# Two-bank projections, key feature sums on TensorE and table loads set by the order, in a gated mix of an S4 convolution and linear attention

## The chip, the cores and the metric

One core of a Trainium2 chip runs the whole program. The metric is the device time of one execution in microseconds (us), of which three runs of the kernel before are given. Engines are named as in the profile: PE (TensorE), DVE (VectorE), ACT (ScalarE), POOL (GpSimd), and SP, whose queue issues nearly all DMAs.

## The reference

Two operators read the same input `x = A_u` (1 x 2048 x 512, bf16) and a gate mixes them. Cut to what is computed:

```python
# A: S4 convolution, per channel d with 128 complex states n
logdA = dt * (A_re + 1j*A_im);  dB = dt * (B_re + 1j*B_im);  Cc = C_re + 1j*C_im
K = einsum("dn,dnl,dn->dl", Cc, exp(logdA[:, :, None] * l), dB).real      # kernel of length 2048
a = irfft(rfft(pad(x)) * rfft(pad(K)))[:2048] + x * Dskip

# B: linear attention, 32 heads of 16 features, "hedgehog" feature map
q, k, v = split(x @ wqkv);  pq = q @ w_phi;  pk = k @ w_phi               # per head
phi = concat([softmax(p), softmax(-p)])                                   # 32 features
num = phi_q @ (phi_k^T v);  den = phi_q . sum_s(phi_k) + 1e-6
b = (num / den) @ wo

g = sigmoid((x * gate_w).sum(-1));   out = g * a + (1 - g) * b
```

## The kernel before, in words

Everything is one program in which each piece of work is a node of a plan (`Plan.add`): an engine, a name, a function that emits its instructions, the nodes that it depends on, and the buffer rings that it takes and drops. `Plan.run` (L153) emits the nodes in a written order. `ORDER` is a string of two-character node numbers, `SIDES` says for each node with a choice whether ACT or DVE does it (evictions of PSUM mostly), and `RINGS` which of two PSUM rings it takes. Each engine executes its instructions in the emitted order; semaphores between engines follow from the tiles.

The work has these stages, which the order interleaves.

1. Tables (`prepare`). Parameters and `x` are loaded on the SP queue; sines and cosines for the Fourier stages (`tgs`, `sine`), transposed `x` (`xps`, `xT`), key and query weights folded with `w_phi` (`wtp`, `wps`, `fold`), and the convolution's tables C, D and G: exponentials `p_d`, `p_ce`, `p_g`, then four rounds of sines (`trig4`: `p_fc` or `p_fd`, `p_ab`, two `p_sn`), joined on DVE (`p_pr`, `p_px`, `p_dd`, `p_de`).
2. Spectrum of `x` (`keys_and_spectrum`): copies `udc`, first stage `psAu` with evictions `XAu`, second stage `psBu` with evictions `XU`, written to DRAM (`xuw`).
3. Keys (`attention_keys`), eight steps `s2` of two token tiles `u`. For each tile `pk` projects the keys into one PSUM bank (128 x 512), two exponentials `ek` (plus and minus) write `Ek`; the sums over the 16 features of each head come either by PE and a DVE reduction or by a DVE reduction alone (`zp`, `zk`, the string `ZPS` chooses; four steps each); `rz` takes the reciprocal as exp(-ln); `vp` projects the values, `vb` evicts them, `vr` multiplies by the reciprocal, and `kn` adds key times value into `kvp`. `kvbd` (L785 to L795) then writes the block-diagonal `KVbd`.
4. Queries (`block`), four blocks of 512 tokens: projection `pq`, exponentials `eq`, sums `zs`, a chain `z1` to `z5`, the weights to DRAM and back, spread over partitions (`aw`, `ar`), multiplication `em` on DVE (L913), `ops` with `KVbd`, eviction `oT`. Blocks 0 to 2 use one-bank tiles of the ring `bk`; block 3 (`late`) runs two banks at a time.
5. Convolution (`plan_conv`), 16 units of 32 channels. Sines `cs` (from `argC`) come in phases of four units with a load of the sine set before and of the exponential set after. Per unit: exponential `E` and its copy `El`, tables A (`A1`, `A2`, and an addition `A3` at L1110 unless `FOURS` has a 1 for the unit, in which case PE adds four terms instead of two), `Rh` and `Rl`, kernel matmuls `kps`, eviction `KD`, Fourier stages `psA`, `psB` with evictions `XA`, `XK`, product `t` (L1231) with the spectrum of `x`, inverse stage `psz`, eviction `Zr`, a turn through DRAM (`zw`, `zr`), last stage `psy`, gating `ou`, and the stores `out`.

[...] The ring `ps` has two tiles of two banks throughout. The other four banks hold `p0` (two wide tiles) in the table stage; then, from the node `x_psum`, the pool `psA` with three one-bank tiles `bk` and one bank `acc`; then, from the node `x_q` (after the last early query block), two wide tiles `pf`. [...]

```python
LN_EXP = "natural_log_exp_and_others"
TRIG = "trig_and_small"
def begin(self, name):                                   # L64
    return self.nc.scalar.preload_act_table_set(name)
```

Loads of a set are nodes of their own here (`tabT`, `tabL`), with dependencies that keep every sine between them.

Of the kernel before, what the change touches and what calls it, by code (L numbers as in the profile page):

```python
# [43 lines left out]
def build_index_cols(nc, pool):  # L44
    idx_i = pool.tile([128, 1], I32, name="idx_i")
    nc.gpsimd.iota(idx_i[:], pattern=[[0, 1]], base=0, channel_multiplier=1)
    want = (("p", 0, 127), ("p31", 0, 31), ("p63", 0, 63), ("h16", 4, 7), ("h2", 4, 1), ("s5", 5, 3), ("b5", 5, 1), ("b6", 6, 1))
# [23 lines left out]
class Plan:  # L71

    DIGITS = "0123456789abcdefghijklmnopqrstuvwxyzABCDEFGHIJKLMNOPQRSTUVWXYZ-_"
    ORDER = ("040B0H0K0d0y0C0D0L0s0I070J0M0P0g000S110j0N08010z0T0m0Q0e2R0a0p0q0r0_0W2T100U0O0V14120Y2U2x0A2S050k130Z2y2V2X2Z0R190v0t0u"
             "0b0c0w2_0l0E0X2W1516172L1a061b2Y022-30311y33340n030f0-"
             "0h1e1f0i1w2J18321c0F0o2B2K2M1n1z1H1g1A1o2D2C1d1p1I091x1E1J351Q1R2F1B0x1C2E0G2H1q36372G2I2P382N2Q391F3b2O3c4C1S3a4J4L4K4M"
             "3d3e4Q4R3f4U1Y3g4N1r4O1h4V3h1L4Y4-"
             "4P3i4Z4_3j4W4S53542z57504T3k4X1Z515b5d58521s1D593l5c3n5i5e55565j3m5a1G3o5q5f5g5s5r5t3p3r3q1T5m5n5u3s5v5h5o5k5w5x5B1P4D4E"
             "3w2v5l5p4F5y5F5C3y1U5H3x5G5I5J5z5A1V5D5E3t3z5U3D5K5V5M5N3A3R3E2w3F5W5L1O5_3G5O5Q5X5Y5Z3B3C1W605R5S1N3K3M1K3S1M5-"
             "5P3L634G642A615T653N673T6869626a666m6n6o3U6p3V3W3X3Y6b6c6q6d6r6s1t3Z3H3-1X3_3O1i1j41401_4221431-"  # L80
             "1k1l204445466e272923222b282d4748243P491m2a4a2c2e4b4g2f4c2g4d252h2o4e4h4i4n1u4j3u3v2j4p2i2l2k2m2q2p6i262s4q4o1v4k2n4u2r2t"
             "6f4v4w6j4r3I2u4x4y4z6g4l8l3J4A8p8m6t6u6k6v8q3Q4f4s6x6h8k8o6l8n8r8s6y6z6w6A6C4m4t4B8C6G8t6I6K8w8x8y8u6B6H6J4H8D8v6L6M6N7d"
             "8z8A8E4I8B7e7f8I7g8F6F9e8Q8G8H9b6O6P8R7h7j7i6Q6R8J9f7M7N8S6S6T6U6Vaeaf7O8W8X8K7k9g8L8T8U8Z8-"
             "938M8N7l6D8_7m8V7n6W6X6Y8O8P8Y7P94an7o7pao7q6_70717r90917Qa47S9295ag7R6Z7s6-"
             "72aha8a9966Ea7akaca5ai73aa75979998ajap7677a69aalatamab74ad7TaBaC7t797u7v7U78au7y7z7V7w7x9caq9naras7AavaH7W9d9h9o9paw7X9v"
             "aY9waK7Y7ZaDaL9q9raZ7a9x9y9zaIc57B7-aM9kc69D9EaQaEbX9L7Cb_aF7D9M7_9Ac07EaRaG9iaxaz80ay9B818285bYaA7Ga-"
             "7IaJ86879j9Fc19s7Jb-"
             "9l9m9Na_7bc7aNaOaPc3cbb2b37HbZc283aS9C7FaT849G9H9I9t89aUaWaV8baX7cccc8c99O9u9P9Q9R888cb87Kb9b0c4caceb19J8abacfcgbg8dck9K"
             "8ecl8f8gbbbh8hbcbibob4cP9Sbpbqcd9T8ichci7L8jcBcCcjcsdYcYctcucycDczdZd-cQcR9Ucmd_cHcvcw9W9Xcnbj9VbwbkblbxcocIbre0eLcp9Ze1"
             "e2b5b6eMbse3eUeVcxb7bye4cqbtbu9Ybdbe9-"  # L90
             "9_cAcrcSbme5cZdOdScEbfcFcGcTcUe6a0a1bve7dTdRdWeNa2e8cJcKe9bzbAedeecLeRcNcOa3eSeaebeOcMc_ePbBd0ecd1d7cVd8d9cWeCdfcXeWdPdU"
             "d2daefege-e_eQd3dbdQdgeTdVd4dndodXdhdcg1g2dieDeEdjeXbKfAbCbnbDbEbFeYfBeZf0f1bGc-dpbLddg7dqbHd5f2drbMf3f4f5bNfGbIbJbOezdk"
             "eAfDdsfEeBeIf6f7feffdldtbPdebQdBfCfHehdueifFejdmf8fgeJd6ekdvfIfJdyf9fafhfbg4fifKg5g6dwfjdzfkfcdxdCdEfLdAdFfMg3g8dGg9dHfN"
             "fleFelfdfmfpdDdLgagbgcgddIeGemeKfqeHfOfPfQfRgeenepfneofreqeresgfggghgifSfTfUfofsbRgjbSgkdJftetglfVfYfZgmgngobUbVgqfufWdM"
             "dNbWgpf-fvfxfygreufwevewexbTeydKfzfXf_g0gvgwgsgtgugx")
    SIDES = ("011111010010101011001110110010011001010100001011100000000000011000011001111101000100000100000000000000000000000010000000"
             "00100001000000000000000101010000000000000100001101001")
    RINGS = ("001010111111010010100000000000000000000000100000000000000000001101100000000101101011100100100001101010111100111001010100"
             "01111")
    WARM = ("000000000000000000000000000000000000000000000000000000000000000000000000000000000000000000000000000000000000000000000000"  # L100
            "000000000000000000000")
    FOURS = ("0111100101011000")
    ZPS = ("01000111")

    HOT = ("pk", "vp", "pq", "zp", "ops", "bps4", "psA", "psBu", "psB128", "psB64", "psB32", "psz", "pszn", "psyn32", "psy128", "psy64", "psy32", "kps")
# [5 lines left out]
    def add(self, eng, name, fn, deps=(), take=(), drop=(), rw=("", ""), tab=None, sets=None, opens=None, cost=0.0):  # L111
        n = Bag()
        n.eng, n.name, n.fn, n.take, n.drop, n.cost = eng, name, fn, list(take), list(drop), cost
        n.tab, n.sets, n.opens, n.ring = tab, sets, opens, None
# [38 lines left out]
    def run(self):  # L153
        code = {d: i for i, d in enumerate(self.DIGITS)}
        order = [64 * code[a] + code[b] for a, b in zip(self.ORDER[0::2], self.ORDER[1::2])] or list(range(len(self.nodes)))
        assert sorted(order) == list(range(len(self.nodes)))
        sides, rings, warm = iter(self.SIDES), iter(self.RINGS), iter(self.WARM)
        for n in self.nodes:
            n.at = n.eng if isinstance(n.eng, str) else n.eng[int(next(sides, 0))]
            for r in n.take:  # L160
                if not isinstance(r, str):
                    n.ring = r[int(next(rings, 0))]
                elif r in self.psums:
                    n.ring = r
            n.warm = int(next(warm, 0)) if n.name in self.HOT and n.ring in ("ps", "bk", "pf") else 0
        done = set()
# [32 lines left out]
def prepare(P, nc, g, evict, psum):  # L199

    fc, act, persist, at = g.fc, g.act, g.persist, g.at
    F = Bag()
# [8 lines left out]
    def S(name, fn, r="", w="", deps=()):  # L211
        return P.add("ACT", name, fn, deps, rw=(r, w))

    t1 = P.add("ACT", "tabT", lambda: act.begin(TRIG), rw=("", "act"), sets="T")
# [57 lines left out]
    def sine(out, v, kv, w, turn=False):  # L272
        S("tgs", lambda: act(out=out(), in_=(low(v()) if not turn else low(v()).rearrange("p (h t) -> p t h", h=2)), func=ACT.Sin, scale=TURN), r="act " + kv, w=w)
# [11 lines left out]
    for hf in range(2):  # L285
# [5 lines left out]
        S("tgs", lambda hf=hf, i=i: act(out=tb(1, hf), in_=F.v[i][:].bitcast(F32), func=ACT.Sin, scale=-1.0, bias=HALF_PI), r=f"act v{i}", w=f"TB1{hf}")  # L291
# [34 lines left out]
    P.add("ACT", "tabL", lambda: act.begin(LN_EXP), [n for n in P.nodes if n.name == "tgs"], rw=("", "act"), sets="L")  # L326
# [4 lines left out]
    S("dtc", dtc, r="act ldc", w="dtc")  # L331
# [49 lines left out]
    S("p_e", lambda: act(out=Tt(4)[:], in_=g.ld_b[:], func=ACT.Exp), r="act ldb tmp", w="t4")  # L381
# [16 lines left out]
    for b in range(8):  # L398
        S("p_d", lambda b=b: act(out=g.D[:, 0, b, :], in_=are(), func=ACT.Exp, scale=64.0 * (b - 3.5)), r="act t2", w=f"D{b}")
    S("p_g", lambda: act(out=g.G[:], in_=are().unsqueeze(2).to_broadcast([128, 512, 2]), func=ACT.Exp, scale=-32.0), r="act t2", w="G")  # L400
    for a in range(4):
        S("p_ce", lambda a=a: act(out=mag()[:, a, :], in_=are(), func=ACT.Exp, scale=512.0 * a + 255.5), r="act t2", w="t7 t8")
    trg = P.add("ACT", "tabT", lambda: act.begin(TRIG), rw=("", "act"), sets="T")
    def trig4(name, fill, r):
# [3 lines left out]
        S("p_sn", lambda: act(out=F.sc[:, 0], in_=X(), func=ACT.Sin, scale=TURN), r="act B0", w="s0")  # L408
        S("p_sn", lambda: act(out=F.sc[:, 1], in_=N(), func=ACT.Sin, scale=-1.0, bias=HALF_PI), r="act B1", w="s1")
# [53 lines left out]
    def at0(e):  # L463
# [4 lines left out]
        e.tensor_scalar(out=at.mask2[:], in0=c8[:, 0:2], scalar1=icol["h2"], scalar2=None, op0=ALU.is_equal)  # L468
# [15 lines left out]
    def at3(e):  # L484
# [8 lines left out]
        e.tensor_copy(out=SZ[:].rearrange("p (m c) -> p m c", m=4)[:, :, 0:32:4], in_=at.mask8[:].unsqueeze(1).to_broadcast([128, 4, 8]))  # L493
# [66 lines left out]
def keys_and_spectrum(P, nc, g, psum):  # L560
# [3 lines left out]
    def bank(name):  # L564
        return g.heat(g.psA.tile([128, 512], F32, name=name, tag="bk"), 2)

# [4 lines left out]
    g.XUn = {}  # L571
    for h in range(2):
# [9 lines left out]
        for g4 in range(8):  # L582
# [17 lines left out]
            a = P.add("PE", "psAu", pa, [a] if g4 else uc, take=["ps"] + (["XAu"] if g4 == 0 else []), drop=(["UDp"] if g4 == 7 else []), rw=("W1", ""))  # L600
            en.append(evict("XAu", ea, [a]))
        eo = []
        for r0 in range(0, 32, 4):
# [26 lines left out]
            a = P.add("PE", "psBu", pb, en + [a], take=["ps"] + (["xst"] if r0 % 8 == 0 else []), rw=(f"TB0{r0 // 16} TB1{r0 // 16} TBn", ""),  # L630
# [25 lines left out]
    sp = P.add("X", "x_psum", shift_psum, [n for n in P.nodes if n.psum is not None and not isinstance(n.psum.take[0], str)], take=["acc"], opens="bk")  # L656
# [969 lines left out]
```

## Time and profile before

| what | value |
|---|---|
| time, median of 3 runs | 265.72 us (265.58 to 268.65) |
| span of the profiled execution (the page gives no other time of it) | 265.4 us |
| PE busy | 208.8 us, 4512 matmuls |
| DVE busy | 233.9 us, 315 instructions |
| ACT busy | 221.7 us, 305 instructions |
| POOL busy | 8.4 us, 21 instructions |
| table loads on ACT | 11 of 1.283 us |
| mean granted TensorE clock | 0.933 |
| DMA | 35.93 MB, mean 135 GB/s |

Busy time of an engine is the union of its instructions. The mean of a group is that of one instruction from start to end; neighbours in a full queue overlap a little, so the group's busy time divided by its count can be less. "Idle before" is how long the engine stood still just ahead of the group's instructions, and on whom it waited.

### The profile page before, as it was taken

To read this page: it belongs to the slowest core of one execution; us is meant where nothing else is said; L and a number is where in the kernel's file an instruction comes from. 1 tells how busy PE (TensorE), PEld (TensorE's weight loads), DVE (VectorE), ACT (ScalarE), POOL (GpSimd) and SP (SyncE) were. 2 spreads that over 40 slices of the span, in tenths; PEclk is the share of its full clock that TensorE was granted. 3 is DMA by queue.
4 is the path that set the end of the run, shared out by engine and by line. 5 is a ranking of instruction groups with operands and counts; after the bars stand their busy time and mean duration, and the time that the engine had idled before them with its cause. 6 is when DMAs were issued, how large, how long until landed. Compare 5 with 4: busy or idle time off the path is not lost.

```text
span 265.4 us, 10071 instructions
## 1 busy us (share of the span) xinstructions
PE 208.8 (79%) x4512; PEld 144.6 (54%) x4512; DVE 233.9 (88%) x315; ACT 221.7 (84%) x305; POOL 8.4 (3%) x21
## 2 busy tenths in 40 slices
PE   0768899999964678898857648999997598999760
PEld 0657556655653424447536336775786167965450
DVE  6798898989799989999999999999999798997630
ACT  6989599899899998989999999999999698763300
POOL 4700000000000000000000000000000000000000
PEclk9986799999997579999999999999999799999985
DMA  7799100155510687203243366239753499898776
GB/s 195 130 198 231 23 0 6 63 155 161 145 39 2 195 243 196 84 4 112 73 158 84 100 233 203 76 119 196 160 176 119 167 227 201 207 173 184 161 115 99
DMA packets 67547, 35.93 MB, mean 135 GB/s; under 512 B 46000, under 2 KB 62000, under 8 KB 67504
## 3 DMA queue, kind: packets, MB, share of 16 engines
q1 hardware_dynamic: 65648, 34.76, 53.4%
q8 instruction: 35, 0.57, 1.0%
q10 hardware_dynamic: 1856, 0.52, 1.0%
q14 instruction: 8, 0.07, 0.1%
HBM read 22.17 MB, written 13.11 MB: 133 GB/s over the span
## 4 chain that ended last, share of the span: by engine, by line
PE 39%; DVE 30%; ACT 11%; DMA 9%; issue 7%; SPq 1%; DVEq 0%; ACTq 0%
PE pk L709 6%; PE vp L757 5%; DVE A L1100 4%; DVE R L1121 3%; DVE R L1117 3%; DVE A L1105 3%; DVE Eq L913 3%; PE kps L183 3%; DMA ZT<-Zd 3%; PE psy L824 3%; DMA wqk<-in_B_wqkv_dram 2%; ACT xst L149 2%; DMA ax<-apd 2%; ACT trg L68 2%; PE psA L591 2%
## 5 line engine op out<-in xcount | busy, mean ns | idle before, releaser
L68 ACT ACTIVATE cs<-args 128x1024 bf16<-128x1024 f32 x32 | 30.9, 1052 | 0.9 <-PE args L1023 0.9
L183 PEld LDWEIGHTS <-A 128*32 128x32 bf16 x1536 | 26.4, 161 | 4.8 <-issue 2.0
L183 PE MATMUL kps<-R,A 128*32 128x64 bf16 x1536 | 27.9, 229 | 1.1 <-DVE R L1121 0.7
L1263 PE MATMUL psz<-t,TI 128*128 128x512 bf16 x60 | 16.7, 412 | 5.4 <-DVE t L1231 4.1
L1121 DVE TENSOR_TENSOR R<-E,cs 128x2048 bf16<-128x2048 bf16 x16 | 19.6, 1222 | 0.1
L1105 DVE TENSOR_TENSOR A<-Ctab,Dtab 128x2048 bf16<-128x2048 bf16 x16 | 19.6, 1223 | 0.0
L1100 DVE TENSOR_TENSOR A<-Ctab,Dtab 128x2048 bf16<-128x2048 bf16 x16 | 19.6, 1222 | 0.0
L1117 DVE TENSOR_TENSOR R<-E,cs 128x2048 bf16<-128x2048 bf16 x16 | 19.5, 1220 | 0.0
L149 ACT CAST Zr<-psz 128x1024 bf16<-128x1024 f32 x15 | 15.2, 1022 | 5.1 <-PE psz L1263 3.6
L68 ACT ACTIVATE Ek<-pk 128x512 bf16<-128x512 f32 x32 | 16.7, 601 | 3.2 <-PE pk L709 3.0
L757 PE MATMUL vp<-WW,xT 128*128 128x512 bf16 x64 | 17.8, 419 | 0.0
L1231 DVE TENSOR_TENSOR t<-XUX,XK 128x2048 bf16<-128x2048 bf16 x14 | 16.8, 1222 | 0.4 <-ACT XK L149 0.4
L68 ACT ACTIVATE E<-args 128x1024 bf16<-128x1024 f32 x16 | 16.4, 1036 | 0.6 <-DVE R L1121 0.5
L68 ACT ACTIVATE Eq<-pq 128x512 bf16<-128x512 f32 (+1 forms) x28 | 16.6, 687 | 0.2
L149 ACT CAST XA<-psA 128x1024 bf16<-128x1024 f32 (+1 forms) x15 | 14.6, 1007 | 2.7 <-PE psA L190 2.7
L616 PE MATMUL psB<-XAu,TB 64*128 64x128 bf16 x256 | 11.7, 249 | 6.3 <-ACT XAu L149 3.1
L709 PE MATMUL pk<-WW,xT 128*128 128x512 bf16 x64 | 16.4, 396 | 0.0
L149 ACT CAST XK<-psB 128x1024 bf16<-128x1024 f32 (+1 forms) x14 | 13.7, 990 | 2.5 <-DVE XK L151 1.3
L843 PE MATMUL pq<-xT,Wqp 128*128 128x512 bf16 x64 | 15.5, 380 | 0.2 <-ACT xT L149 0.2
L616 PEld LDWEIGHTS <-TB 64*128 64x128 bf16 x256 | 9.5, 110 | 10.0 <-issue 9.9
L190 PE MATMUL psA<-W,KD 128*64 128x128 bf16 x256 | 9.8, 221 | 5.0 <-ACT cs L68 2.9
L65 ACT ACT_TABLE_LOAD x10 | 12.8, 1283 | 0.1
(211 smaller groups left out, 506.9 us busy)
## 6 DMA issues: line engine op xcount, KB each, us to landing
XUX<-XUd SPq DMA_DIRECT2D x32, 256.0 KB
XUd<-xst SPq DMA_DIRECT2D x8, 512.0 KB
ax<-apd SPq DMA_DIRECT2D x16, 256.0 KB
Zd<-Zr SPq DMA_DIRECT2D x15, 256.0 KB
ZT<-Zd SPq DMA_DIRECT2D x6, 512.0 KB
UD<-in_A_u_dram SPq DMA_DIRECT2D x16, 128.0 KB
XUd<-xst SPq DMA_DIRECT2D x8, 256.0 KB
wqk<-in_B_wqkv_dram SPq DMA_DIRECT2D x1, 1024.0 KB
```

The source lines that it names most:

```text
L68: return self.nc.scalar.activation(**kw)
L149: self.nc.scalar.copy(out=o, in_=i)
L183: nc.tensor.matmul(kps[32 * dj:32 * dj + 32, g4, e, :], lhsT=A[:, ka, :, :, d].rearrange("p a b -> p (a b)"), rhs=R[:, kr, d, :], start=(i ...
L616: nc.tensor.matmul(box.ps[:, c2, sl, :], lhsT=fc.TB[rows, b0:b0 + 2].rearrange("p a b -> p (a b)"), rhs=X.t[rows, k, r0 + sl].rearrange("p ...
L709: nc.tensor.matmul(box.ps[:], lhsT=xT[:, st, kt, :], rhs=g.WW[:, kt, :], start=(kt == 0), stop=(kt == 3))
L757: nc.tensor.matmul(box.ps[:], lhsT=xT[:, st, kt, :], rhs=g.WW[:, 4 + kt, :], start=(kt == 0), stop=(kt == 3))
L1100: nc.vector.tensor_tensor(out=c.A[:, 0:2].rearrange("p o a b c -> p (o a) b c"), in0=g.C[U // 8][:, 0:2, :, d0 % 256:d0 % 256 + 32].rearra ...
L1105: nc.vector.tensor_tensor(out=c.A[:, 2:4].rearrange("p o a b c -> p (o a) b c"), in0=g.C[U // 8][:, 1:3, :, d0 % 256:d0 % 256 + 32].rearra ...
L1117: nc.vector.tensor_tensor(out=c.R[:, :, :, 32:64], in0=t.E[:, 1].unsqueeze(1).to_broadcast([128, 2, 32, 32]), in1=t.cs[:], op=ALU.mult)
L1121: nc.vector.tensor_tensor(out=c.R[:, :, :, 0:32], in0=t.E[:, 0].unsqueeze(1).to_broadcast([128, 2, 32, 32]), in1=t.cs[:, ::-1, :, ::-1], o ...
L1231: nc.vector.tensor_tensor(out=box.t, in0=Ls[r0 // ns].X[:], in1=box.XK[:].unsqueeze(1).to_broadcast([128, 2, 1024]), op=ALU.mult)
L1263: nc.tensor.matmul(box.ps[:, hb, :], lhsT=fc.TI[:, k].rearrange("p t h a -> p (t h a)"), rhs=box.t[:, k, 512 * hb:512 * hb + 512], start=( ...
```

## The change

It has five parts.

- **Projections.** `pk` and `vp` fill two banks for both token tiles of a step (`pk2`, `vp2`); one exponential of each sign, one value eviction, one `vr2` and one `kn2` serve 1024 columns. Query blocks 0 to 2 use the two-bank form that block 3 has. The three `bk` banks become one wide tile `b2` and one bank `bk`; keys, spectrum, gate and early queries choose between `ps` and `b2`.
- **Key sums.** `w_phi` is written so that features of a pair of heads alternate; every step's sums are 16 matmuls of 128 columns with the identity, and `rz` reads them in PSUM. `zk` and `ZPS` are gone. Masks and the layout of the query weights (`apd`, `ax`) follow the head pairs: `aw` becomes two DMAs, `ar` reads 4 KB rows to every second partition.
- **Table sets.** `tabT` and `tabL` are gone; `run` loads a set where the next ACT node's set differs from the one held. By the new order this happens 18 times. `PHASES` is gone: sines come by pairs of units.
- **FOURS** has fourteen ones instead of eight (units 13 and 15 are the zeros).
- **Order.** `ORDER`, `SIDES` and `RINGS` are new. Among the evictions, ACT has 8 `XU` for 12, 7 `XAu` for 8, 7 `KD` for 10, 1 `udc` for 3. `sel1` moves from DVE to POOL. On SP, `wqk` comes after `Bim`, `Bre`, `Are`, the two step-size loads and `Aim`; before, it came second. `x_q` comes earlier among the convolution units. The repeated heating matmuls (`WARM`, all zeros before) are removed.

```diff
-    FOURS = ("0111100101011000")
-    ZPS = ("01000111")
+    FOURS = ("1111111111111010")
...
+            if n.at == "ACT" and n.tab and n.tab != held:
+                held = n.tab
+                self.load_set(held)
             n.fn()
...
+    P.load_set = lambda k: act.begin(TRIG if k == "T" else LN_EXP)
...
     def at1(e):
         at.Wphi = g.kpool.tile([128, 4, 128], BF16, name="Wphi")
-        e.tensor_tensor(out=at.Wphi[:].rearrange("p m (h f) -> p m h f", h=8), in0=g.wc[:].unsqueeze(2).to_broadcast([128, 4, 8, 16]),
-                        in1=at.mask8[:].unsqueeze(1).unsqueeze(3).to_broadcast([128, 4, 8, 16]), op=ALU.mult)
+        for h2 in range(2):
+            e.tensor_tensor(out=at.Wphi[:].rearrange("p m (r f h) -> p m r f h", r=4, h=2)[:, :, :, :, h2], in0=g.wc[:].unsqueeze(2).to_broadcast([128, 4, 4, 16]),
+                            in1=at.mask8[:, h2::2].unsqueeze(1).unsqueeze(3).to_broadcast([128, 4, 4, 16]), op=ALU.mult)
...
+    key2 = ("ps", "b2")
...
-            a = P.add("PE", "psAu", pa, [a] if g4 else uc, take=["ps"] + ...
+            a = P.add("PE", "psAu", pa, [a] if g4 else uc, take=[key2] + ...
...
+        def pk(s2=s2, box=box):
+            box.ps = psum([128, 2, 512], "pk")
+            for u in range(2):
                 for kt in range(4):
+                    nc.tensor.matmul(box.ps[:, u, :], lhsT=xT[:, 2 * s2 + u, kt, :], rhs=g.WW[:, kt, :], start=(kt == 0), stop=(kt == 3))
+        def ex(K=K, box=box):
+            K.E = g.kwk.tile([128, 2, 2, 512], BF16, name="Ek")
+            for sg in range(2):
+                act(out=K.E[:, :, sg, :], in_=box.ps[:], func=ACT.Exp, scale=(1.0 if sg == 0 else -1.0))
...
+        def ps4(K=K, box=box):
+            box.ps = psum([128, 2, 2, 32], "zk")
+            o = box.ps[:].rearrange("p u g h -> p (u g h)")
+            e = K.E[:].rearrange("p u g (b f h) -> p (u g b) f h", f=16, h=2)
+            for f in range(16):
+                nc.tensor.matmul(o, lhsT=g.ident[:], rhs=e[:, :, f, :], start=(f == 0), stop=(f == 15), skip_group_check=True)
+        def rc(K=K, box=box):
+            K.v = g.kwk.tile([128, 2, 2, 17, 32], BF16, name="vr")
+            act(out=box.ps[:], in_=box.ps[:], func=ACT.Ln)
+            act(out=K.v[:, :, :, 16, :], in_=box.ps[:], func=ACT.Exp, scale=-1.0)
+        z = P.add("PE", "zp", ps4, red, take=["bk"])
+        l = P.add("ACT", "rz", rc, [z], take=["vr"], drop=["psum"], tab="L")
...
         def aw():
-            nc.sync.dma_start(out=g.apd[b].rearrange("i h m c -> (i h m) c"), in_=Q.apm[:].rearrange("p s t -> p (s t)"))
+            for ip in range(2):
+                nc.sync.dma_start(out=g.apd[b, ip].rearrange("h m i c -> i (h m) c"), in_=Q.apm[64 * ip:64 * ip + 64].rearrange("p s t -> p (s t)"))
...
-            for i in (2 * ip, 2 * ip + 1):
-                nc.sync.dma_start(out=Q.ax[:, i].rearrange("p m s t -> p (m s t)"),
-                                  in_=g.apd[b, i].rearrange("h m c -> h (m c)").unsqueeze(1).to_broadcast([8, 16, 1024]))
+            for h in range(2):
+                nc.sync.dma_start(out=Q.ax[h::2, ip].rearrange("p m i s t -> p (m i s t)"),
+                                  in_=g.apd[b, ip].rearrange("(r h) m i c -> h r (m i c)", h=2)[h].unsqueeze(1).to_broadcast([4, 16, 2048]))
...
-                      "KD": 1, "XA0": 1, "XK": 2, "Zr": 2, "XUX": 3, "ln": 8}, {"ps": 2, "p0": 2, "bk": 3, "acc": 1, "pf": 2})
-        g.P, g.PHASES, g.nxst = P, {0: 4, 4: 8, 8: 12, 12: 16}, P.k["xst"]
+                      "KD": 1, "XA0": 1, "XK": 2, "Zr": 2, "XUX": 3, "ln": 8}, {"ps": 2, "p0": 2, "b2": 1, "bk": 1, "acc": 1, "pf": 2})
```

More of the change, by code (lines that the diff above doesn't have):

```diff
@@ L164, in run @@
                     n.ring = r
-            n.warm = int(next(warm, 0)) if n.name in self.HOT and n.ring in ("ps", "bk", "pf") else 0
-        done = set()
+        done, held = set(), None
         for i in order:
@@ L771, in kn @@
+        def kn(s2=s2, K=K):
+            for u in range(2):
                 for i in range(8):
@@ L832, in block @@
         a = None
-        nm = 2 if late else 1
-        for m0 in range(0, 4, nm):
+        ring = psq if late else key2
+        for m0 in range(0, 4, 2):
             box = Bag()
@@ new lines, in block, with po_ @@
+            box = Bag()
+            def po_(ip=ip, box=box):
+                if late and ip == 0:
+                    g.Wqp = None
+                    w = g.aq.tile([128, 2, 4, 256], BF16, name="oT3", tag="Wqp")
+                    g.oT[3] = [w[:, i] for i in range(2)]
+                box.ps = psum([128, 2, 512], "ops")
+                for m in range(4):
+                    for sg in range(2):
+                        c = 256 * (m % 2)
+                        nc.tensor.matmul(box.ps[:, m // 2, c:c + 256], lhsT=at.KVbd[:, 4 * sg + m, :],
+                                         rhs=Q.e[:, 2 * ip:2 * ip + 2, m, sg, :], start=(sg == 0), stop=(sg == 1), skip_group_check=True)
+                if ip == 1:
+                    Q.e = None
@@ L1003, in shift_q @@
         g.shift_queries()
-    sq = P.add("X", "x_q", shift_q, bs_n + g.gate + [n for n in P.nodes if n.psum is not None and "bk" in n.psum.take], opens="pf")
+    sq = P.add("X", "x_q", shift_q, bs_n + g.gate + [n for n in P.nodes if n.psum is not None and ("bk" in n.psum.take or key2 in n.psum.take)], opens="pf")
     r.update(bs=bs_n, sq=sq, block=block)
@@ L1397, in plan_conv @@
     for h in range(6):
-        for u in (2 * h, 2 * h + 1):
-            if u in g.PHASES and u:
-                phase(range(u, g.PHASES[u]))
+        sines((2 * h, 2 * h + 1))
         if h % 2 == 0:
```

290 lines of the change are left out of this document (106 added, 184 removed).

## The prediction

> **What bounds the kernel now.** I read the busy totals first, then the span cut into stretches by what the kernel does, then the groups of instructions by form, and last the chain of work. A stretch's row gives its length, then busy us (and count) of PE, PEld, DVE, ACT and POOL, the granted TensorE clock and the DMA share.
>
> ```profile
> PE 208.8 (79%) x4512; PEld 144.6 (54%) x4512; DVE 233.9 (88%) x315; ACT 221.7 (84%) x305; POOL 8.4 (3%) x21
> ```
> ```profile
> 0.00:32.00 32.00, 19.08 (x165) 15.80 (x166) 25.57 (x58) 25.67 (x32) 8.36 (x21) 0.84 0.82 161
> 32.00:75.00 43.00, 42.34 (x757) 26.22 (x755) 37.30 (x52) 39.27 (x77) 0.00 (x0) 1.00 0.30 86
> 75.00:106.00 31.00, 20.85 (x306) 12.19 (x306) 29.98 (x50) 30.01 (x32) 0.00 (x0) 0.78 0.49 139
> 106.00:196.00 90.00, 74.72 (x1830) 52.23 (x1827) 89.69 (x104) 87.93 (x121) 0.00 (x0) 1.00 0.45 125
> 196.00:240.00 44.00, 37.54 (x952) 28.68 (x950) 40.55 (x40) 33.88 (x37) 0.00 (x0) 0.96 0.77 187
> 240.00:265.40 25.40, 14.23 (x524) 9.53 (x516) 10.83 (x16) 4.91 (x10) 0.00 (x0) 0.84 0.74 131
> ```
> The bound changes hands. From 32 to 75 us, most of the key projections, TensorE is full (42.3 of 43). From 75 to 106, the trigonometry of the tables, ACT and DVE are full (30.0 of 31 each) and TensorE has a third of its time free at a clock of 0.78. From 106 to 196, convolution with queries, DVE is full and ACT at 98%. From 240 on nothing is full: a chain of short dependent steps and DMAs.
>
> ```profile
> L736 DVE TENSOR_REDUCE Zk<-Ek 128x64 f32<-128x1024 bf16 x8 | 9.3, 1210 | 0.0
> L739 DVE TENSOR_REDUCE Zk<-zk 128x128 f32<-128x512 f32 x4 | 2.8, 692 | 1.7 <-PE zk L730 1.6
> L730 PE MATMUL zk<-Ek,ident 128*128 128x256 bf16 x32 | 4.2, 277 | 0.0
> L1110 DVE TENSOR_TENSOR A<-A 128x2048 bf16<-128x2048 bf16 x8 | 9.8, 1224 | 0.1
> L65 ACT ACT_TABLE_LOAD x10 | 12.8, 1283 | 0.1
> L68 ACT ACTIVATE Ek<-pk 128x512 bf16<-128x512 f32 x32 | 16.7, 601 | 3.2 <-PE pk L709 3.0
> L68 ACT ACTIVATE Eq<-pq 128x1024 bf16<-128x1024 f32 x4 | 3.8, 1030 | 0.1
> L68 ACT ACTIVATE cs<-args 128x1024 bf16<-128x1024 f32 x32 | 30.9, 1052 | 0.9 <-PE args L1023 0.9
> ```
> Here are the prices: busy over count is what one costs in a full queue, since neighbours overlap by some 0.09 us (cs: 30.9 / 32 = 0.966, not 1.052).
>
> **The change part by part.** I read the new order string against the node numbers that the planning functions give out, so that each engine's list and each eviction's side is known.
>
> Table loads. The rule "load when the held set differs" gives 18 loads in the new ACT list; with the one ahead of the first copy, 19 for 11. None falls differently before the first key exponential (3 and 3), 4 more come among the keys (6 for 2: the sines of the tables now sit between key exponentials), 4 more after them (10 for 6). In the timeline a load starts 0.02 us after the instruction ahead ends and the next starts 0.01 after the load, so it costs its 1.283 and the lost overlap, 1.37: +11.0 us of ACT, 5.5 in each part.
>
> [...]
>
> Wide projections. 32 exponentials of 512 at 0.522 become 16 of 1024 at 0.966: 16.7 to 15.5, -1.2. The early queries' 24 of 512 (12.8) become 12 at 0.95: -1.4. Per 1024 evicted, one instruction takes the place of two: ACT's key value evictions go from 7 x 0.6 to 2 x 0.95 (-2.3), DVE's from 9 x 0.62 to 6 x 1.14 (+1.2), and scaling by `vr` from 16 to 8 (-1.1 on DVE).
>
> Key sums. All reductions leave DVE: 9.3 + 2.8 = -12.1 us. TensorE sums 16 features of both token tiles in 16 matmuls of 128 columns per step: 2048 columns, as many as a step of today's 8 matmuls of 256 (0.92 us). Four steps did it, now eight: +3.7 by columns; by instructions, 128 at 0.115 less the 3.7 now spent, +11. The 128-column `psB` matmuls (7.0 / 96 = 0.073) give 9.3 - 3.7 = +5.6. I take +4, nearer the columns, since one stationary matrix serves all.
>
> FOURS. Fourteen units for eight skip the add L1110: six fewer at 1.14 in a full queue, -6.8 on DVE. Each doubles its kernel matmuls from 64 (1.14 us on the chain) to 128 (2.2 to 2.3): +6.6 on TensorE.
>
> Sides. Of the first convolution stage's evictions (XU) four go from ACT to DVE: -3.9 and +4.6; one XAu: -1.0 and +1.1; UDp copies 3 to 1 on ACT: -1.9 and +0.7; KD: -1.9 and +2.2; the rest, in ones and twos, gives ACT +1.2 and DVE -2.0. The selection matrix leaves DVE (-1.2) for GpSimd; by its 512-wide rows (1.04 and 1.50) it takes 2 to 3 us there, hidden by some 50 us to its first reader. That cover gone, argC would be late and the sines with it.
>
> DMAs. `aw` is two issues instead of one: four more at 0.41 on SP, ahead of `ar` in the same queue, so the weights land up to 0.8 us later. `ar` keeps its count and bytes, in 4 KB instead of 2 KB rows to every second partition; no row shows that. Bounds: it lands 1 us earlier or 2 later than the 5.9 us on the chain. What waits is `em` on DVE, 1.7 us in the late block; I take 0 since the new order puts about as much DVE work ahead of it (some 10 us). At the start `wqk` goes from second to after five 128 KB loads and the step sizes. Its landing held the first transposes until 7.9 us; 640 KB ahead at that slice's 195 GB/s makes them 3.3 us later. ACT and DVE have the step sizes and sines to do meanwhile. Bounds 0 and +3; I take +1.
>
> **The sum, by stage.** Totals are ACT 221.7 to about 220, DVE 233.9 to about 221, TensorE 208.8 to about 219: three engines level.
> Start (0 to 32): +1.
> Keys (32 to 106, 74 us): TensorE 42.3 + 20.9 + 4 = 67.2; ACT 69.3 + 5.5 - 1.2 - 2.3 - 3.9 - 1.0 - 1.9 = 64.5; DVE 67.3 - 12.1 - 1.1 + 1.2 + 4.6 + 1.1 + 0.7 - 1.2 = 60.5. The order mixes the sines among the projections, so TensorE need not idle while ACT and DVE work. As full as now from 32 to 75 (98%) it is 68.5 us; three coupled queues do worse, and I take 69: -5. Bounds -6 and 0 without a new wait.
> Convolution and queries (106 to 240, 134 us): DVE 130.2 - 6.1 = 124.1; ACT 121.8 + 5.5 - 3.0 = 124.3; TensorE 112.3 + 6.6 = 118.9. DVE alone was 97% full; now two are equal and TensorE close. 128 at 97%, 138 if they hinder one another to 90%; I take 132, nearer the first: -2.
> Tail: 25 us, the same chain; 0.
> Sum -6 against the span of 265.4, which lies 0.3 us below the median of 265.72 (the page gives no other time of that execution): 259.4, and 259.7 beside the median; I say 259.5.
>
> **The rivals.**
> Everything relieved counts. DVE's idle time stays at 265.4 - 233.9 = 31.5 us and its work is 221: 252.5. For it: the early query blocks end sooner in the new order (x_q, which turns their banks into two more wide tiles for the convolution, comes with 81 us of ACT work left by the rows' means, not 59). Against: ACT, at 98%, loses nothing after the keys. Some 253.
>
> Relief off the path. ACT takes over as the bound after the keys with ten loads, and the keys stay at 73: 265.4 + 1 - 1 - 1 = 264.4. For it: 87.9 of 90 on ACT already. Against: -5 there needs only that free TensorE time from 75 to 106 be used.
>
> Wide tiles starve TensorE, the slower side. Key stage and spectrum share three two-bank tiles (two of `ps`, one of `b2`). Without waiting, a pk tile is held 3.1 us (filled from 41.3, last exponential done at 44.4), vp as long, psAu 0.87 + 1.2 + 0.3 = 2.4, psBu 1.9, four argC 2.6, two gate tiles 2.5: 16 x 3.1 + 16 x 2.4 + 16 x 1.9 + 10.4 + 5 = 134 tile-us, 45 us on three. Over 69 us each of 54 tiles can wait (207 - 134) / 54 = 1.35 us for its evicting engine. Beyond that the stage grows by 18 us per us of mean wait: at 2.4 us, (134 + 130) / 3 = 88, +14 on today's 74 and some 278 with the rest. For it: ACT and DVE each work through one list in order and are 90% full, so two instructions of 1 us ahead are common. Against: by the same working today's two wide tiles leave 1.7 us each, and TensorE is full from 32 to 75.
>
> A switch costs more than its row, because work of one set queued behind a sine that is not ready stands still with it. At a load's own 1.3 us again for each of eight: 259.5 + 10 = 270 where all fall on the path. Against: ACT waited 0.1 us in all ahead of ten loads. [...]
>
> **How the numbers follow.** Forecast 0.42, everything counts 0.20, off the path 0.21, starved tiles 0.13, switches 0.04. Two per cent, about what a measurement of this kernel tells from no change, is 260.4 below and 271.0 above. Two thirds of the forecast's case lie below 260.4 (0.28), with the second case 0.48; starved tiles, half the switches and the upper end of the third give 0.17 slower; 0.35 remains. The range reaches to the first rival with its bound (start 0, keys -6, tail -1) at 251, and up past the switches to 272, leaving most of the starved case out.
>
> **What would show it.** Right: 19 loads, 1.28 each; DVE near 221, ACT near 220, TensorE near 219; no Zk reduction on DVE; KVbd written at 102 instead of 106; 106-to-240's counterpart near 132 with ACT and DVE both above 93%. Wrong: TensorE's pk, vp or psA matmuls waiting for ACT or DVE by several us in all (starved tiles); zk matmuls over 1.2 us a step; sizable waits ahead of loads; a first key exponential later than 33 us; a tail longer than 26.

## The result, and the profile after

The changed kernel takes **298.84 us** (median; 297.95 to 302.88), the kernel before 265.65 us beside it. The ratio is 1.126 with an interval of 1.118 to 1.134: slower by 33 us, where 259.5 was forecast with 272 as the upper end. Here and below a time is the median of all executions, while a ratio compares undisturbed ones only, since some executions run a few per cent longer. The profiled execution has a span of 297.5 us and a mean granted TensorE clock of 0.906 (0.933 before).

The page after, its busy totals and the first two rows of the chain of work that ended last:

```profile
PE 223.8 (75%) x4974; PEld 163.9 (55%) x4992; DVE 224.7 (76%) x292; ACT 223.4 (75%) x268; POOL 11.1 (4%) x24
...
PE 38%; DMA 23%; DVE 18%; ACT 9%; issue 6%; SPq 5%; DVEq 0%; ACTq 0%
DMA ax<-apd 18%; PE zk L715 4%; PE psz L1226 4%; PE kps L175 4%; PE pk L699 4%; PE vp L730 3%; PE psy L798 3%; PE pq L817 2%; DMA Aim<-in_A_A_im_dram 2%; SPq L878 2%; DMA XUd<-xst 2%; SPq L350 2%; DVE R L1084 2%; DVE A L1068 2%; PE psA L582 1%
```

The work is level over three engines, close to the forecast's totals (220, 221 and 219 for ACT, DVE and PE), and each is busy for three quarters of the span. One group of transfers, the read of the query weights into `ax`, makes 18% of the chain. The groups after that answer to the prices shown before:

```profile
L65 ACT ACT_TABLE_LOAD x18 | 23.1, 1283 | 0.3
L715 PE MATMUL zk<-Ek,ident 128*128 128x128 bf16 x128 | 15.4, 287 | 0.0
L885 DVE TENSOR_TENSOR Eq<-Eq,ax 128x2048 bf16<-128x2048 bf16 x8 | 9.8, 1226 | 26.0 <-DMA ax<-apd 26.0
```

The last column is idle time of the engine just ahead: 18 loads (the nineteenth has a line of its own) cost their 1.283 us each and 0.3 us of waiting in all; the key sums cost 15.4 us of TensorE where four steps cost 4.2; VectorE stood still for 26.0 us ahead of eight products `Eq`. The stretches, cut at the time when `KVbd` is written, first of before, then of after (length, busy us and count of PE, PEld, DVE, ACT, POOL, clock, DMA share, GB/s):

```profile
34.00:106.40 72.40, 61.58 (x1053) 37.41 (x1052) 65.65 (x99) 67.72 (x105) 0.00 (x0) 0.91 0.39 111
106.40:170.00 63.60, 49.30 (x1279) 33.84 (x1278) 63.36 (x75) 62.13 (x89) 0.00 (x0) 1.00 0.35 113
```
```profile
34.00:106.40 72.40, 65.03 (x1140) 47.12 (x1145) 57.12 (x72) 63.35 (x84) 0.00 (x0) 0.97 0.29 82
106.40:170.00 63.60, 45.09 (x1136) 30.89 (x1135) 47.79 (x60) 50.08 (x62) 0.00 (x0) 0.88 0.32 96
```

`KVbd` is written at 106.4 us in both kernels. All of the loss comes behind it: 297.5 - 106.4 = 191.1 us for 265.4 - 106.4 = 159.0. In the first 64 us of that, VectorE falls from full to 47.8 of 63.6 and ScalarE to 50.1. VectorE's waits and the pieces of the chain (start, us, what) say for what:

```profile
DVE Eq L885 <- DMA ax<-apd: 26.0, 8, 4.4
DVE xT L1329 <- PE psy L1304: 5.2, 2, 3.2
```
```profile
126.43 12.95 DMA ax<-apd
148.56 13.09 DMA ax<-apd
164.74 13.66 DMA ax<-apd
220.36 12.66 DMA ax<-apd
```

Each of the four query blocks has one piece of some 13 us; before, one piece stood on the chain in the whole span:

```profile
201.09 5.91 DMA ax<-apd
```

All eight products wait: VectorE works through its list in order (in the timeline it starts nothing in the 2.91 us ahead of the first product and the 3.88 us ahead of the second), and the list has too little ahead of them. The stall also reaches TensorE, which stood idle from 138 to 142 us, around the end of the first of these pieces; its granted clock from 140 to 149 us was 0.50 (the third number from the end):

```profile
140.00:149.00 9.00, 5.38 (x82) 3.68 (x85) 8.68 (x14) 4.28 (x8) 0.00 (x0) 0.50 0.22 70
```

### The profile page after: what moved, and what is told of

Its sections match the earlier page's. It is cut to its first block, busy times and chain, and to the rows that moved or that the text cites. A ratio compares the mean times of both kernels' runs of the same rounds, so it can differ in the third digit from the quotient of the medians.

```text
span 297.5 us, 10975 instructions
## 1 busy us (share of the span) xinstructions
PE 223.8 (75%) x4974; PEld 163.9 (55%) x4992; DVE 224.7 (76%) x292; ACT 223.4 (75%) x268; POOL 11.1 (4%) x24
## 4 chain that ended last, share of the span: by engine, by line
PE 38%; DMA 23%; DVE 18%; ACT 9%; issue 6%; SPq 5%; DVEq 0%; ACTq 0%
DMA ax<-apd 18%; PE zk L715 4%; PE psz L1226 4%; PE kps L175 4%; PE pk L699 4%; PE vp L730 3%; PE psy L798 3%; PE pq L817 2%; DMA Aim<-in_A_A_im_dram 2%; SPq L878 2%; DMA XUd<-xst 2%; SPq L350 2%; DVE R L1084 2%; DVE A L1068 2%; PE psA L582 1%
## 5 line engine op out<-in xcount | busy, mean ns | idle before, releaser
L175 PE MATMUL kps<-R,A 128*32 128x64 bf16 x1920 | 34.9, 232 | 9.9 <-DVE R L1084 5.8
L175 PEld LDWEIGHTS <-A 128*32 128x32 bf16 x1920 | 32.9, 160 | 13.5 <-issue 5.4
L885 DVE TENSOR_TENSOR Eq<-Eq,ax 128x2048 bf16<-128x2048 bf16 x8 | 9.8, 1226 | 26.0 <-DMA ax<-apd 26.0
L139 ACT CAST XA<-psA 128x1024 bf16<-128x1024 f32 x14 | 13.9, 1023 | 5.5 <-PE psA L182 5.5
L903 PE MATMUL ops<-Eq,KVbd 128*128 128x256 bf16 x64 | 10.8, 326 | 9.5 <-DVE Eq L885 8.3
L68 ACT ACTIVATE Eq<-pq 128x1024 bf16<-128x1024 f32 x16 | 15.4, 1044 | 0.8 <-PE pq L817 0.8
L68 ACT ACTIVATE Ek<-pk 128x1024 bf16<-128x1024 f32 x16 | 15.3, 1026 | 0.7 <-PE kvp L748 0.5
L715 PE MATMUL zk<-Ek,ident 128*128 128x128 bf16 x128 | 15.4, 287 | 0.0
L699 PE MATMUL pk<-WW,xT 128*128 128x512 bf16 x59 | 14.6, 379 | 1.2 <-DVE xT L141 0.8
L730 PE MATMUL vp<-WW,xT 128*128 128x512 bf16 x61 | 14.8, 380 | 0.6 <-DVE XAu L141 0.4
```

Source lines behind the costliest of these rows:

```text
L68: return self.nc.scalar.activation(**kw)
L139: self.nc.scalar.copy(out=o, in_=i)
L175: nc.tensor.matmul(kps[32 * dj:32 * dj + 32, g4, e, :], lhsT=A[:, ka, :, :, d].rearrange("p a b -> p (a b)"), rhs=R[:, kr, d, :], start=(i ...
L699: nc.tensor.matmul(box.ps[:, u, :], lhsT=xT[:, 2 * s2 + u, kt, :], rhs=g.WW[:, kt, :], start=(kt == 0), stop=(kt == 3))
L715: nc.tensor.matmul(o, lhsT=g.ident[:], rhs=e[:, :, f, :], start=(f == 0), stop=(f == 15), skip_group_check=True)
L730: nc.tensor.matmul(box.ps[:, u, :], lhsT=xT[:, 2 * s2 + u, kt, :], rhs=g.WW[:, 4 + kt, :], start=(kt == 0), stop=(kt == 3))
```

## The experiments

**Which property of the read.** The outermost dimension of a read is the first and slowest one of its access pattern: here the source rows, each of which is then repeated for 16 partitions; the variant with outermost 16 puts the repetition first. Before, a read fills all 128 partitions from 8 rows (outermost dimension 8); after, every second partition from 4 rows. Theory O: outermost 4 lets few of the DMA engines work. Rival S: every second partition is slow in itself. For the key sums, theory G: TensorE pays for reading two neighbours at a time with gaps between; rival W: loading `ident` 16 times a step is the bound. Four kernels answer.

Neighbouring partitions, outermost still 4:
```diff
-nc.sync.dma_start(out=Q.ax[h::2, ip]...
+nc.sync.dma_start(out=Q.ax[64 * h:64 * h + 64, ip]...
```


> The changed kernel, but each of the two weight loads (ar) writes 64 neighbouring partitions instead of every second one; bytes, rows of 4 KB, number of issues and the outermost dimension of the source (4) stay. The weights land on the wrong heads' partitions, so the attention part of the output is wrong. Theory O (the outermost dimension of 4 lets few DMA engines work): nothing changes, a pair of loads still takes some 5 us, DVE still waits about 26 us for ax, time 297 to 301 us. Theory S (writing every second partition is slow): a pair takes 2 to 3 us, DVE waits under 6 us for ax, time 268 to 276 us.

307.5 us, ratio 1.146 [1.140, 1.153]: no gain at all, so S falls. Theory O had expected no change; that it is 2% slower still than after (1.126) is not explained.

Outermost 16, four reads for each half block instead of two:
```diff
-for h in range(2):
-    nc.sync.dma_start(out=Q.ax[h::2, ip]..., in_=...[h].unsqueeze(1).to_broadcast([4, 16, 2048]))
+for r in range(4):
+    nc.sync.dma_start(out=Q.ax[32 * r:32 * r + 32, ip]..., in_=....unsqueeze(0).to_broadcast([16, 2, 2048]))
```


> The changed kernel with each pair of weight loads written as four, one per 32 partitions, with the 16-fold repetition as outermost dimension; same bytes, same rows, same place, two issues more per pair (0.54 us each on SP). Both O and S expect fast landing, since the partitions are neighbours too: DVE's wait for ax falls from 26 to under 6 us and the time to 268 to 276 us (298.8 less 26 and what the product and its matmuls wait behind it). A third theory, that the DMAs are only the messenger and the table loads and wide tiles set the time, expects under 5 us gained: 294 us or more.

278.92 us, ratio 1.048 [1.040, 1.055]: 20 of the 33 us are gone. Before with its reads cut into outermost 4, same bytes, same rows:
```diff
-for i in (2 * ip, 2 * ip + 1):
-    nc.sync.dma_start(out=Q.ax[:, i]..., in_=....to_broadcast([8, 16, 1024]))
+for h in range(2):
+    for i in (2 * ip, 2 * ip + 1):
+        nc.sync.dma_start(out=Q.ax[64 * h:64 * h + 64, i]..., in_=....to_broadcast([4, 16, 1024]))
```


> The kernel before with each of its weight loads cut in two halves of 64 partitions, so that the outermost dimension of the source is 4 instead of 8; same bytes, rows of 2 KB as before, twice the issues (8 instead of 4 a block). Theory O: a quarter of the engines at most, DVE waits for ax 15 us or more where it waited 1.7, time 275 to 290 us. Theory S: the partitions are neighbours, so only the four more issues a block on SP show, time 265 to 269 us.

271.41 us, ratio 1.021 [1.013, 1.030]: the direction of O, but less than I had expected of it (15 us of waits or more). VectorE's waits for `ax`, first with outermost 16 in the new order, then with outermost 4 in the old:

```profile
DVE Eq L885 <- DMA ax<-apd: 2.6, 3, 1.3
```
```profile
DVE Eq L914 <- DMA ax<-apd: 9.1, 3, 4.7
```

Outermost 4 costs 9.1 us of waits in the old order and 26.0 in the new. In the old its pieces on the chain are 9.0 to 10.2 us instead of some 13, and five of the eight products find their weights there in time. So the loss has two parts, the form of the read and the lack of cover.

How much of the DMA engines works is in the traces too. The last two numbers of these rows are the mean busy share of the 16 DMA engines and the GB/s, while by the timeline of issues only this read is under way: after (outermost 4), before (8) and the version with four repairs that comes further down (16, with 8 KB rows).

```profile
132.00:139.00 7.00, 3.39 (x136) 3.05 (x129) 1.23 (x1) 4.23 (x6) 0.00 (x0) 1.00 0.26 103
```
```profile
123.00:127.00 4.00, 4.00 (x195) 3.53 (x188) 3.97 (x7) 3.97 (x8) 0.00 (x0) 1.00 0.54 199
```
```profile
139.30:140.30 1.00, 1.00 (x50) 0.89 (x48) 1.00 (x2) 1.00 (x2) 0.00 (x0) 1.00 0.92 303
```

Of 16 engines these shares make 4.2, 8.6 and 14.7, close to the outermost dimension each time, and the rate rises with them: theory O holds, as far as a mean share can tell. The pieces on the chain agree: with rows of 4 KB some 13 us at outermost 4 and 2.7 to 4.2 at 16, with rows of 2 KB 9.0 to 10.2 at 4 and 5.9 at 8, though before's form took 6.8 to 9.1 us in versions of the new order.

**The key sums.** After with 128 neighbouring columns in each matmul of the sum (other columns than the sum needs, which changes values only):
```diff
-rhs=e[:, :, f, :]
+rhs=e[:, 128 * f:128 * f + 128]
```


> The changed kernel with the 16 key-sum matmuls of a step reading 128 neighbouring columns each, instead of pairs of columns at a step of 32; the key sums, and so the attention part, are wrong; count, columns and weight loads stay. Theory G (the gaps in the moving operand halve TensorE's reading): a step falls from 1.75 to 0.9 us, TensorE's busy time by some 7 us, keys end 3 to 6 us earlier, time 293 to 296 us. Theory W (each matmul of 128 columns is bound by its own load of the 128 x 128 identity, about 0.1 us): a step stays at 1.7 us and the time at 297 to 300 us.

294.44 us, ratio 1.107 [1.100, 1.115]. The groups after and here:

```profile
L715 PE MATMUL zk<-Ek,ident x128: 268/287/306, 37.8 to 88.3; 128*128 128x128 bf16 x128
```
```profile
L715 PE MATMUL zk<-Ek,ident x128: 219/219/230, 40.2 to 83.9; 128*128 128x128 bf16 x128
```

Same count, same columns, same stationary matrix: 287 ns become 219 (shortest, median and longest are given), busy time falls from 15.4 to 8.5 us, and from the first sum to `KVbd` it takes 61.9 us instead of 68.6. G holds, W falls.

**Both at once, and what is left.** After with before's transfers (one write and four reads a block, outermost 8):
```diff
-for ip in range(2):
-    nc.sync.dma_start(out=g.apd[b, ip]..., in_=Q.apm[64 * ip:64 * ip + 64]...)
+nc.sync.dma_start(out=g.apd[b]..., in_=Q.apm[:]...)
...
+for i in (2 * ip, 2 * ip + 1):
+    nc.sync.dma_start(out=Q.ax[:, i]..., in_=....to_broadcast([8, 16, 1024]))
```


> The kernel after, with the query weights' transfers of the kernel before: one write of 128 rows and four reads a block with outermost dimension 8 and 2 KB rows, in place of two writes and four reads of outermost 4. Weights land on other heads, which changes values only. Theory T (the transfers alone make the loss that is not the key sums'): the waits of the Eq products for ax fall from 26.0 us to under 4, the write's landing to about 1.5 us, and the time to 268-274 us, below the 278.9 of the version with outermost 16, because SP issues 4 reads a block of about 0.6 us instead of 8. Rival R (the new order and the two-bank tiles cost some 8 us by themselves): 276-281 us, no better than the version with outermost 16.

278.54 us, ratio 1.039 [1.030, 1.047], as with outermost 16 and as rival R had it: SP's four saved issues a block bring nothing that shows. And with the neighbouring columns too:

> The same and the key sums' matmuls on 128 neighbouring columns (the sums are of other columns, which changes values only). Theory T: both named costs are gone, so what is left is the forecast's sum with the price it took for the key sums: 259-266 us. Rival R (order and tiles): 271-277 us, and the stage before KVbd is then shorter by some 4 us while the stage from there to the end stays over 165 us against before's 159.

Ratio 1.014 [1.006, 1.023], that is 269.9 us as the ratio counts (the median is 273.64). Theory T, that only the two named costs stood between forecast and result, falls: `KVbd` comes at 99.9 us, 6.5 sooner than before, but from there to the end it takes 267.0 - 99.9 = 167.1 us against 159.0. These 8 us rest on one profiled execution each, and in four runs that leave before's key stage as it is `KVbd` came at 104.1 to 106.4 us, so some 2 us of them are uncertain. Two causes were tried, a third was read. First, before's FOURS string in this version:
```diff
-FOURS = ("1111111111111010")
+FOURS = ("0111100101011000")
```


> The version with the transfers of before and the key sums' matmuls on neighbouring columns (269-271 us, KVbd at 99.9 us, 167.1 us from there to the end against before's 159.0), and the FOURS string of before in place of after's: 8 units with four terms instead of 14. Its key sums are of other columns, which changes values only. Theory F (TensorE's extra terms hold A, of which there is one buffer, and come late on TensorE): the stage from KVbd to the end falls to 158-162 us and the time to 261-265 us; VectorE's waits for kps and psy together fall from 14.9 us by at least 6. Rival R (the new order with its seven further table loads behind KVbd makes the stage long): the stage stays within 2 us of 167, time 268-272 us.

271.53 us, ratio 1.028 [1.019, 1.036], 267.7 - 100.0 = 167.7 us behind `KVbd`: taking FOURS back alone does not shorten it, as rival R had it (though the loads behind `KVbd` are four more, 10 for 6, not seven). Second, no table loads in the convolution, in both orders:
```diff
-act(out=T.cs[:, 0], in_=i, func=ACT.Sin, ...)
+act(out=T.cs[:, 0], in_=i, func=ACT.Exp, ...)
```


> The kernel before with the sines of units 4 to 15 computed as exponentials, and without the table loads around them (values differ; same instructions else): 4 loads instead of 11. By the run with twice the loads (0.97 us a load, 8.6 us longer behind KVbd): 257-261 us, 152-155 us behind KVbd. Rival (loads cost only when added to this order): 263-266 us.

> The version with the transfers of before and the key sums on neighbouring columns (269-271 us, KVbd at 99.9 us, 167.1 us behind it), and all sines of the convolution as exponentials without table loads around them (values differ): 4 loads instead of 19. Theory L (the further loads make what is left): behind KVbd it takes as long as the kernel before without switches, within 2 us, some 153-156 us, and KVbd comes some 5 us earlier, time 250-258 us. Rival R (the order): still 6 us or more longer behind KVbd than before without switches, time 259-264 us.

No load is left behind `KVbd` in either run (6 and 9 fewer; 5 and 10 are left in all, not 4). Before without them: 265.76 us, ratio 1.002 [0.997, 1.007], 158.6 us behind `KVbd`: the rival holds. The mended version without them: 274.78 us, ratio 1.039 [1.030, 1.048], 272.2 - 98.8 = 173.4 us behind `KVbd`, although ScalarE has 10.6 us less to do (210.9 for 221.5). Theory L falls; why it takes longer than with the loads is not shown. Adding loads, on the other hand, costs:
```diff
 def begin(self, name):
+    self.nc.scalar.preload_act_table_set(LN_EXP if name == TRIG else TRIG)
     return self.nc.scalar.preload_act_table_set(name)
```


> The kernel before with the other table set loaded ahead of each load of a set: 22 loads instead of 11, the same work else. The forecast put each further load on ScalarE at 1.37 us and, where ScalarE keeps the pace, on the path: 11 loads, 15 us of ScalarE, time +8 to +14 us. Rival (loads fall where ScalarE waits for others anyway, or their price is hidden): less than +4 us.

276.4 us, ratio 1.043 [1.038, 1.049]. The first of before's 11 loads does not pass through this function, so that there are 21 loads and not 22: ten more (ScalarE 234.4 us for 221.7), some 11 us, about 1.1 us a load. The 0.97 in an expectation above was reckoned with eleven.

Third, the order itself. It was read, not tried: a new order was not built. Times are starts in the timeline, less the start of `KVbd`:

| us behind `KVbd` | before | mended (both repairs) | after |
|---|---|---|---|
| last `Eq` product of the three early blocks | 64.4 | 54.3 | 72.1 |
| last `Eq` product of the late block | 104.7 | 103.3 | 126.7 |
| last table product `R` | 131.3 | 142.0 | 166.0 |
| end of the span | 159.0 | 167.1 | 191.1 |

VectorE's groups from the last `Eq` product on, first of before, then of the mended version:

```profile
L1100 DVE TENSOR_TENSOR A<-Ctab,Dtab 128x2048 bf16<-128x2048 bf16 x3 | 3.7, 1220 | 0.0
```
```profile
L1062 DVE TENSOR_TENSOR A<-Ctab,Dtab 128x2048 bf16<-128x2048 bf16 x4 | 4.9, 1216 | 0.0
```

There is one product of this line for each unit of 32 channels. The new order does the early queries 10 us sooner, and has four units of the convolution left when the last query block is through, where before has three. They pass one after the other (last `Eq` to last `R`: 38.7 us for four, 26.6 for three, 9 to 10 us a unit), with the other engines waiting in turn. That fits the 8 us, but no run isolates it, nor what came with the order: the new `SIDES` and `RINGS` and the two-bank tiles of the early query blocks.

**The forecast's reliefs, one at a time in before's own order.** All eight key sums on TensorE in before's form, and the opposite:
```diff
-ZPS = ("01000111")
+ZPS = ("11111111")
```


> The kernel before with all eight key steps summed by TensorE first (runs of 4 neighbours, 0.92 us a step) and a quarter-size VectorE reduction, in its own order. Forecast's reading (VectorE is relieved on the path): VectorE loses the four full reductions (12.1 us of the forecast's sum, less the four quarter ones), KVbd comes 1-5 us earlier, time 261-266 us. Rival (order set for the other split, ScalarE bounds the stage): KVbd within 1 us of 106.4, time within 1 us of before.

274.02 us, ratio 1.021 [1.011, 1.031]; `KVbd` at 110.3 instead of 106.4, about as much later as the four added steps cost (4 x 0.92 = 3.7), which neither theory had. VectorE, relieved of four full reductions, stands and waits for the sums instead, first before, then here:

```profile
DVE Zk L739 <- PE zk L730: 1.6, 3, 1.1
```
```profile
DVE Zk L739 <- PE zk L730: 9.0, 7, 2.7
```

With `ZPS = ("00000000")`:

> The kernel before with all eight key sums reduced by VectorE, none by TensorE first: TensorE 4 times 0.92 us less, VectorE some 4 times 2.4 us more. All eight on TensorE put KVbd from 106.4 to 110.3 us. Theory T (TensorE's time is on the path of the key stage one for one): KVbd at 102-104 us, time 261-264 us. Rival W (VectorE has no room, or any other split than the order's own costs): KVbd at 106 us or later, time 265-272 us.

272.12 us, ratio 1.023 [1.011, 1.036], `KVbd` at 108.9: no better, as rival W had it. After's FOURS string in before, and the opposite:

> The kernel before with the FOURS string of after (14 of 16 units with four terms by TensorE instead of 8): VectorE 6.8 us less, TensorE 6.6 us more by the forecast's rows. If VectorE's share of the conv stage is on the path (busy 97% there): 260-264 us. Rival (ScalarE, as busy, keeps the pace, or TensorE comes late in the tail): 265-270 us.

272.27 us, ratio 1.022 [1.016, 1.028]. VectorE's busy time fell by 5.8 us (233.9 to 228.1; the sum had 6.8), and the time rose by 6, more than either theory had: `A` has one buffer, and the next unit's product now waits until the doubled matmuls have read it (here, then before):

```profile
L1100 DVE TENSOR_TENSOR A<-Ctab,Dtab 128x2048 bf16<-128x2048 bf16 x16 | 19.5, 1222 | 6.1 <-PE kps L183 6.0
```
```profile
L1100 DVE TENSOR_TENSOR A<-Ctab,Dtab 128x2048 bf16<-128x2048 bf16 x16 | 19.6, 1222 | 0.0
```

With no unit of four terms:

> The kernel before with no unit of four terms instead of 8: TensorE some 8 times 1.1 us less, VectorE 8 times 1.14 us more. Fourteen units of four terms instead of 8 made 272.3 us. Theory T (TensorE's kps is on the path behind KVbd): 257-263 us. Rival W (VectorE is busy 97% behind KVbd, so 9 us more of it come out at the end): 268-276 us.

274.19 us, ratio 1.033 [1.027, 1.040]. Both directions of both switches cost 2 to 3% (the intervals together span 1.011 to 1.040). Where VectorE gets more work, the time grows by about that work: 5.7 us more (239.6) without key sums on TensorE, 9.2 more (243.1) without four terms. Where it gets less, the waits shown above take more than the relief. Both fit rival W, that the order is written for its own split; a list rewritten for another split was not run.

**A version with four repairs**, meant to beat both: before's FOURS, eight matmuls a step over runs of four neighbours with a VectorE addition, reads of outermost 16 with 8 KB rows, the write in four.
```diff
-for f in range(16):
-    nc.tensor.matmul(o, lhsT=g.ident[:], rhs=e[:, :, f, :], ...)
+for f in range(8):
+    nc.tensor.matmul(box.ps[:, 0:256], lhsT=g.ident[:], rhs=e[:, :, f, :], ...)
+nc.vector.tensor_reduce(out=box.ps[:, 256:384]..., in_=box.ps[:, 0:256]..., axis=mybir.AxisListType.X, op=ALU.add)
```


> After with four repairs: FOURS of before; key sums by eight matmuls a step over runs of four neighbours (256 columns) and a VectorE addition of the pairs; the ax read as four transfers a block, one for each 32 partitions, outermost dimension 16 and 8 KB rows; the apd write as four of outermost 8. By theory F, a key sum at before's 0.92 us a step, and 2-3 us of waits for ax: KVbd at 101-103 us, a stage of 159-163 us behind it, time 262-267 us. By rival R: 270-275 us.

292.74 us, ratio 1.099 [1.090, 1.109], far from both theories. The addition sits in VectorE's list at a place that the order doesn't foresee, and five times it holds up all behind it:

```profile
DVE zk L715 <- PE zk L714: 15.9, 5, 5.5
```

`KVbd` comes at 116.7 us, and the reads, of which the first product needs all four, made VectorE wait 9.5 us. No version that I ran beats before.

## Why the prediction was wrong

**The read of the weights: the step that failed most.** The prediction put that `ar` "keeps its count and bytes", bounded its landing at 1 us earlier or 2 later, and took 0. The bounds came from no row, only from the nearest transfer's time; "every second partition" was seen, and that the outermost dimension thereby falls from 8 to 4 was not priced. At outermost 4 the DMA engines were busy to 0.26 and moved 103 GB/s, before 0.54 and 199. Measured: 26.0 us of waits on VectorE, and 20 us of the time when the form is mended in either way. The cover named for it, "about as much DVE work ahead of it", was not there.

**Key sums: the wrong size, by a cause that the sum left out.** +4 was taken of bounds +4 to +11, "nearer the columns, since one stationary matrix serves all". It was 15.4 - 4.2 = +11.2 us, the end that I had set aside. But the reason given for that end, a price by instructions, is not the cause: with neighbouring columns as many instructions make the term 8.5 - 4.2 = +4.3, my value. What the sum left out is that pairs of columns are read with gaps between. With neighbouring columns `KVbd` comes at 99.9 us, somewhat better than the 102 forecast, and that is in part luck. From 32.8 us to there ScalarE (63.6 us) and VectorE (57.7) have nearly the forecast's work (64.5 and 60.5), but TensorE is busy for 60.0 of 67.1 us, 89%, where 67.2 us of work at 98% was forecast: less work and looser packing cancel. The overrun of some 7 us took all that the stage had won.

**Convolution: 132 us were taken for 134, "nearer the first".** Here two sums of busy time were treated as if the order would pack them. The work itself came nearly as summed; the counterpart of the stretch in the version with both repairs, up to 25.4 us before its end, is:

```profile
99.90:241.60 141.70, 121.21 (x3142) 89.11 (x3142) 127.89 (x139) 125.47 (x144) 0.00 (x0) 0.96 0.60 154
```

VectorE has 127.9 us and ScalarE 125.5 (124.1 and 124.3 forecast), in 141.7 us instead of 132: full to 90% and 89%, the case of "138 if they hinder one another to 90%" that was set aside. FOURS gave VectorE and TensorE nearly what was said (-5.8 us; 34.8 for 27.9 us of `kps`), and in before's order that alone was a loss. With the two other errors mended, the stretch behind `KVbd` is 8 us longer than before instead of 2 shorter. Neither FOURS nor the loads, taken back one at a time, make it shorter; the order, with what came with it, is what remains. That it is the cause is argued from the reading above and not shown.

**Table loads: count and price right.** 19 loads, 1.283 us each, 0.3 us of waits; ten stand behind `KVbd`, and of the six put among the keys one already comes ahead of the first key exponential, at 31.4 us. Ten more in before's order cost about 1.1 us each, so that +11.0 us of ScalarE was not far off as an addition; but leaving them out brought nothing in either order, so they don't explain the loss.

The rival by which a switch costs more than its row, 1.3 us again for each of eight, falls by the waits: 0.3 us in all ahead of 18 loads and 0.1 ahead of the 32 sines.

**The other rivals.** Neither of the two that weighed VectorE's relief (all of it counts, or none does) priced what the single changes in before's order showed, a loss. The starved tiles did not come: in the key stage TensorE's `pk` waited 0.8 us in all, `vp` 0.4 and `psA` 0.6; only `psB` of the spectrum waited 4.1 (6.3 before). It was key sums, not tiles, that filled the stage. The signs listed were right: `zk` over 1.2 us a step was among them (15.4 / 8 = 1.9). A wait for `ax` was not listed, because its cost had been put at 0. The first key exponential came at 32.8 us as said (32.0 before).

The three errors, in the time: 298.8 to 276.5 with before's transfers, to 269.9 with neighbouring columns, to 259.5 forecast: 22, 7 and 10 us. The first two were each found by a run that changes nothing else in the kernel after; of the third only the place and the packing are known.

## What to carry to other kernels

Of a transfer that a change reshapes, compare the outermost dimension, old and new, ahead of its bytes and its count, and ask what work a list in fixed order has ahead of its first reader: here 20 of 33 us sat there. A relief of a busy engine counts only if the order uses it: four changes of durations in an order written out for others each cost 2 to 3% here, so price a relief in the order that will carry it. For a matmul whose moving operand (the streamed one) is newly read with gaps, price the gaps: here 0.120 us a matmul (15.4 / 128) instead of 0.066.

## What the runs showed of the hardware

Two neighbouring elements at a time (4 bytes, 64 bytes apart) cost TensorE 15.4 us for 128 matmuls of 128 columns, neighbouring columns 8.5, with nothing else changed. Reads with outermost dimension 4, 8 and 16 (rows of 4, 2 and 8 KB, one window of a profile each) kept the 16 DMA engines busy to 0.26, 0.54 and 0.92 and moved 103, 199 and 303 GB/s. With 4 they took some 13 us on the chain where those with 16 took 2.7 to 4.2, at equal bytes in all, and it made no gain whether the 64 partitions lay side by side or every second one.
